# First sequence's softmax by token and its mix on TensorE, w_r loaded behind q, low parts of w_v and half of w_k made by accumulating transfers

## The chip, the cores and the metric

The kernel runs on one core of one Trainium2 chip. The metric is the device time of one execution in microseconds; a kernel's time is the median of several runs. Five engines work at once, each on its own instructions in a fixed order: TensorE (PE in the profile, with its weight loads as PEld), VectorE (DVE), ScalarE (ACT), GpSimd (POOL) and SyncE (SP), which issues most of the DMA transfers. They wait for each other by semaphores.

## The reference

Eight sequences of 576 tokens, eight heads of 64 channels. Each sequence has 32 packed queries `p`; an attention of `p` over `k` and `v` gives 32 packed values per head, and a second attention of `q` over these packed values gives the output of the attention. Its heads side by side are the 512 channels of `x`, which goes through a channel mix with a shift by one token.

```python
p_packed = sm_attn(p, k, v)               # softmax over 576 keys
x = sm_attn(q, p_packed, p_packed)        # softmax over 32 packed rows, (8, 576, 512)
x_prev = x shifted by one token, zero first
xk = mu_k * x + (1 - mu_k) * x_prev
xr = mu_r * x + (1 - mu_r) * x_prev
k = max(xk @ w_k, 0)                      # 512 -> 1024
v = k * k @ w_v                           # 1024 -> 512
out = 1 / (1 + exp(-(xr @ w_r))) * v
```

`mu_k`, `mu_r`, `w_k`, `w_v` and `w_r` come as 64-bit floats, the rest as 32-bit floats.

## The kernel before

**Order of work.** The kernel is written as generators ("parts") that yield what they need next: an engine with an estimated duration, a buffer slot, or an event. While the program is built, `Flow.run` takes the part that can start soonest by these estimates and, among equals, the one of lowest rank, and writes its instruction down. So each engine has a fixed order, made by a planner; on the chip only semaphores decide when an instruction starts. Ranks: 10 and up for the first sequence (less 1 for its second half), `RANK_MIX` 11.5 for the first block's mix, `RANK_W` 13.6 for w_r and w_k, 14.28 for the second sequence, `RANK_V` 15.2 for w_v, 30 and up for later sequences, 50 for the channel mix.

**Weights.** TensorE multiplies float32 in three products of rounded parts: high by high, high by low, low by high. `convert` (L268) brings one chunk of 128 rows by 512 columns of 64-bit words (512 KB) into a staging slot and makes the two parts: ACT reads the upper word (L286), DVE shifts and joins it with sign and lower word (L288, L290, L292), ACT rounds it to the high part (L296), DVE subtracts that from the word (L298) to get the low part. There are 4 chunks of w_r, 8 of w_k (columns 0 to 511 first, then 512 to 1023), 8 of w_v. Staging slots are borrowed from `sq`, at most four at a time (`staged`). The word lies in one of four `tmp` buffers until both parts are made.

**Attention.** For each sequence `loads` brings k, v and q in, four pairs of heads each. The first two sequences are transposed on TensorE (L394), later ones on DVE (L371). `front` (L435) computes the scores of `p` (L444), softmax (`weights_of`), the sum over v (L486 or L478) and `pm`, the packed values (L501). `back` (L617) does the second attention in two halves of 288 tokens: scores on TensorE (L611) with packed rows on partitions, a transpose on DVE in blocks of 32 (L635), maximum, subtraction, exponential, sum, reciprocal and product (L642 to L654), a transpose back (L658), and the product with `pm` (L666), copied by ACT to `xt` (L688), channels on partitions.

**Channel mix.** Tokens of all sequences in blocks of 512; block 0 holds tokens 0 to 511 of the first sequence, block 1 its last 64 and 448 of the second. `mix` (L707) makes xr or xk for 4 chunks of 128 channels: ACT multiplies `xt` by the share (L721), DVE multiplies the shifted `xt` and adds (L725); `split` rounds (ACT, L741) and subtracts (DVE, L743). Then on TensorE, per block: `gates` (48 matmuls of 128x512, L799 to L801, four token tiles, the next block's xr and all of w_r needed), `keys` (96, L760 to L762, eight groups f of 128 hidden channels, each over four chunks of xk and w_k), `squared` on ACT and DVE (L771 to L780), `values` (96, L828 to L830). `keep_busy` puts filler matmuls (L899) where TensorE would idle by plan, until the last gate tile of block 0. PSUM has two slots `pa` of two banks for the attention, and four slots `m` of one bank, of which one is the fillers' until then.

**Loads.** All go through SP in the planner's order (L207). The first two w_r chunks have ranks just behind the first sequence's loads (`FIRST`). `shares` (L869) loads `mu_k` and `mu_r`, one value per partition and chunk (L871), and makes one minus them (L875).

## Time and profile before

| what | value |
|---|---|
| median of 3 runs | 598.3 us (597.15 to 598.65) |
| the profiled execution's own time | 602.04 us |
| its span, first to last instruction | 600.3 us |
| mean granted TensorE clock | 0.997 |
| PE, PEld, DVE, ACT, POOL busy | 587.6, 465.4, 372.3, 317.4, 2.1 us |
| DMA traffic | 56.51 MB, 94 GB/s over the span |

One profiled execution gives all starts and durations. A row of the timeline has the start from the span's beginning, the duration, engine, line, operation, output and inputs, shapes and count; in brackets the idle time before it and what ended that. A row of groups has count, busy time, mean nanoseconds of one, and idle time before. Matmuls overlap their successors, so their durations add up to more than the time they take; their starts tell the pace. Four stages can be told apart: up to 44 us the first sequence and the weights, to 61 us the first block's gates, to 118 us its keys and values beside the second sequence, and then eight more blocks with the other sequences between them.

### The profile page before, as it was taken

The numbers are of one execution on the slowest core, as the hardware profiler recorded it, in microseconds if no ns is written. First come the engines' busy times: TensorE is split into PE (matmuls) and PEld (weight loads), VectorE is DVE, ScalarE is ACT, GpSimd is POOL, SyncE is SP. The second block draws the span as 40 slices with busy tenths as digits, with TensorE's granted clock in tenths as the row PEclk, the third lists the DMA queues.
The fourth block names the chain that finished last, engine by engine and source line by source line (L and its number), as shares of the span: only waits on it lengthen the run. The fifth ranks groups of instructions, "written<-read, shape, count | busy, mean of one in ns | idle before, by whom it ended". The sixth has DMA issues, their size and how long they took to land.

```text
span 600.3 us, 10117 instructions
## 1 busy us (share of the span) xinstructions
PE 587.6 (98%) x3924; PEld 465.4 (78%) x3924; DVE 372.3 (62%) x713; ACT 317.4 (53%) x555; POOL 2.1 (0%) x23
## 2 busy tenths in 40 slices
PE   9999999999999999998999999999999999999997
PEld 8777677787777777676777787778788888888886
DVE  1499999966779769745962977186404812551321
ACT  3578784863585675543833575257524703631410
POOL 0000000000000000000000000000000000000000
PEclk9999999999999999998999999999999999999999
DMA  8894661674665760764636343200100010001001
GB/s 194 250 281 120 218 149 42 141 168 84 143 135 130 155 137 15 186 142 70 133 82 166 89 77 93 79 0 1 58 13 1 1 70 1 0 1 70 1 0 71
DMA packets 170895, 56.51 MB, mean 94 GB/s; under 512 B 147808, under 2 KB 162144, under 8 KB 170848
## 3 DMA queue, kind: packets, MB, share of 16 engines
q1 hardware_dynamic: 170848, 55.87, 38.1%
q8 instruction: 31, 0.51, 0.3%
q14 instruction: 16, 0.13, 0.1%
HBM read 42.86 MB, written 12.98 MB: 93 GB/s over the span
## 4 chain that ended last, share of the span: by engine, by line
PE 80%; DVE 6%; SPq 5%; DMA 4%; ACT 2%; issue 2%; ACTq 0%; DVEq 0%
PE pvo L828 11%; PE pvo L830 11%; PE pvo L829 11%; PE ph L760 10%; PE ph L762 9%; PE ph L761 9%; SPq L207 5%; PE pr L799 4%; PE pr L801 4%; PE pr L800 4%; PE pa L666 2%; DVE m L290 2%; PE pa L611 1%; PE pa L478 1%; DMA vt<-in_v 1%
## 5 line engine op out<-in xcount | busy, mean ns | idle before, releaser
L760 PE MATMUL ph<-xk,wk_h 128*128 128x512 f32 x288 | 115.2, 400 | 0.0
L828 PE MATMUL pvo<-wv_h,sq 128*128 128x512 f32 x288 | 114.0, 396 | 0.0
L761 PE MATMUL ph<-xk,wk_h 128*128 128x512 f32 x288 | 112.7, 391 | 0.0
L762 PE MATMUL ph<-xk,wk_l 128*128 128x512 f32 x288 | 112.7, 391 | 0.0
L829 PE MATMUL pvo<-wv_l,sq 128*128 128x512 f32 x288 | 112.2, 390 | 0.0
L830 PE MATMUL pvo<-wv_h,sq 128*128 128x512 f32 x288 | 112.1, 389 | 0.0
L771 ACT ACTIVATE r<-ph 128x512 f32<-128x512 f32 x72 | 43.1, 598 | 93.5 <-PE ph L762 92.4
L778 DVE CAST sq<-r 128x512 fp32r<-128x512 f32 x72 | 30.2, 419 | 92.3 <-ACT r L774 89.9
L828 PEld LDWEIGHTS pvo<-wv_h,sq 128*128 128x128 f32 x288 | 54.0, 188 | 17.2 <-issue 6.3
L760 PEld LDWEIGHTS ph<-xk,wk_h 128*128 128x128 f32 x288 | 54.2, 188 | 16.2 <-issue 5.2
L725 DVE SCALAR_TENSOR_TENSOR x<-xt,mus,x 128x512 f32<-128x512 f32 (+7 forms) x128 | 60.4, 510 | 6.4 <-ACT x L721 6.2
L762 PEld LDWEIGHTS ph<-xk,wk_l 128*128 128x128 f32 x288 | 54.3, 189 | 11.6
L830 PEld LDWEIGHTS pvo<-wv_h,sq 128*128 128x128 f32 x288 | 54.1, 188 | 11.5
L829 PEld LDWEIGHTS pvo<-wv_l,sq 128*128 128x128 f32 x288 | 54.1, 188 | 10.7
L761 PEld LDWEIGHTS ph<-xk,wk_h 128*128 128x128 f32 x288 | 54.3, 188 | 10.3
L721 ACT ACTIVATE x<-xt,mus 128x512 f32<-128x512 f32 (+7 forms) x128 | 61.5, 528 | 1.3 <-DVE xr L743 1.3
L801 PE MATMUL pr<-wr_h,xr 128*128 128x512 f32 x144 | 56.5, 393 | 1.0 <-DVE xr L743 1.0
L799 PE MATMUL pr<-wr_h,xr 128*128 128x512 f32 x144 | 56.8, 395 | 0.0
L800 PE MATMUL pr<-wr_l,xr 128*128 128x512 f32 x144 | 56.1, 390 | 0.0
L810 ACT ACTIVATE sig<-pr 128x512 f32<-128x512 f32 x36 | 21.5, 600 | 60.5 <-PE pr L801 60.4
L780 DVE TENSOR_TENSOR sq<-r,sq 128x512 fp32r<-128x512 f32 x72 | 49.3, 685 | 1.4
L774 ACT ACTIVATE r<-r 128x512 f32<-128x512 f32 x72 | 45.5, 631 | 1.7
(85 smaller groups left out, 681.3 us busy)
## 6 DMA issues: line engine op xcount, KB each, us to landing
out<-sig SPq DMA_DIRECT2D x36, 256.0 KB, 2.5
vt<-in_v SPq DMA_DIRECT2D x16, 512.0 KB, 4.5
raw<-in_k SPq DMA_DIRECT2D x96, 72.0 KB, 2.7
raw<-in_q SPq DMA_DIRECT2D x96, 72.0 KB, 2.8
st<-in_moe_w_k SPq DMA_DIRECT2D x8, 512.0 KB, 6.2
st<-in_moe_w_v SPq DMA_DIRECT2D x8, 512.0 KB, 5.6
far<-at SPq DMA_DIRECT2D x12, 288.0 KB, 2.3
aTd<-far SPq DMA_DIRECT2D x12, 256.0 KB, 2.9
```

Of the source, the lines that this page charges most:

```text
L721: nc.scalar.mul(x32[:, o:o + n], xts[b, c][:, 1 + s:1 + s + n], mus[:, j, c:c + 1])
L725: nc.vector.scalar_tensor_tensor(x32[:, o:o + n], xts[b, c][:, s:s + n], mus[:, j + 1, c:c + 1], x32[:, o:o + n], op0=ALU.mult, op1=ALU.add,)
L760: nc.tensor.matmul(ph, wk_h[:, c, fs], xh, start=(c == 0), stop=False)
L761: nc.tensor.matmul(ph, wk_h[:, c, fs], xl, start=False, stop=False)
L762: nc.tensor.matmul(ph, wk_l[:, c, fs], xh, start=False, stop=(c == NC - 1))
L780: nc.vector.tensor_tensor(hl[:, 1, :], r, hl[:, 0, :].bitcast(F32), op=ALU.subtract)
L799: nc.tensor.matmul(pr, xh[:, ts_], wr_h[:, c, :], start=(c == 0), stop=False)
L800: nc.tensor.matmul(pr, xh[:, ts_], wr_l[:, c, :], start=False, stop=False)
L801: nc.tensor.matmul(pr, xl[:, ts_], wr_h[:, c, :], start=False, stop=(c == NC - 1))
L828: nc.tensor.matmul(pv[t], sh, wv_h[:, f, :], start=(f == 0), stop=False)
L829: nc.tensor.matmul(pv[t], sh, wv_l[:, f, :], start=False, stop=False)
L830: nc.tensor.matmul(pv[t], sl, wv_h[:, f, :], start=False, stop=(f == NF - 1))
```

## The change

It concerns the start of the kernel.

- **By token.** The first sequence's second attention is computed with tokens on partitions (`by_token`): q is the stationary operand, `both` holds the packed rows of a pair of heads on the diagonal, and the scores of 128 tokens come as 256 columns. `weights_by_token` does the softmax in windows of 256, 256 and 64 tokens without the DVE transposes, then transposes on TensorE and copies to `A0`, with a zero column ahead.
- **Mixed on TensorE.** `shared` multiplies `pm` by the shares of each channel and by one minus them; `first_mix` then gets xr and xk directly as two accumulated products, of `A0` and of `A0` one token earlier. ACT rounds from PSUM, DVE subtracts from PSUM, 256 columns at a time. The last 64 tokens are kept in float32 for block 1 (`kept`), where `mix` copies them.
- **Gates of block 0** run two token tiles side by side over the chunks, so they need only the first 256 tokens at first; the fillers end ahead of the second two.
- **Loads.** All four chunks of w_r come right behind the first sequence's q; the staging area is a pool `st` of eight slots of its own, without the limit of four. The parts of w_v stay in these slots. The q of the first sequence goes through `sq` slots. The shares are loaded by POOL's queue, once repeated over 32 partitions for `shared`, and later by rows with a transpose on TensorE for the other blocks.
- **Low parts by transfer.** For w_v and the second half of w_k the subtraction L298 goes: ACT writes minus the high part, and a transfer from POOL's queue adds the word to it in place.
- **Waits.** w_k's conversion waits for the third window; the third sequence's front waits for the second sequence's `px`.

The core of the diff:

```diff
-    FIRST = 10.09, 10.29
+    FIRST = 10.05, 10.06, 10.07, 10.08
...
-                pa=2, both=1, m=4, staged=4)
+                pa=2, both=1, m=4, st=NF)
...
-        staged = yield from flow.take("staged")
-        slot = yield from flow.take("sq")
+        slot = yield from flow.take("st")
...
+        if held:
+            yield from flow.wait(("A", 2))
...
         nc.vector.scalar_tensor_tensor(m, w0, 29, m, op0=ALU.logical_shift_right, op1=ALU.bitwise_or)
-        flow.give("sq", slot)
-        flow.give("staged", staged)
+        if hi is None:
+            wv = wvs[c] = tile_([P, 2, DM], F32R, "st", slot, "wv")
+            h, l = wv[:, 0, :], wv[:, 1, :]
+        else:
+            h, l = hi[:, c, o:o + n], lo[:, c, o:o + n]
+            flow.give("st", slot)
         yield act(n)
-        nc.scalar.copy(hi[:, c, o:o + n], m.bitcast(F32))
-        yield vec(n)
-        nc.vector.tensor_tensor(lo[:, c, o:o + n], m.bitcast(F32), hi[:, c, o:o + n].bitcast(F32), op=ALU.subtract)
+        nc.scalar.copy(h, m.bitcast(F32))
+        if event[0] == "wk" and o or event[0] == "wv":
+            yield act(n)
+            nc.scalar.activation(l, h.bitcast(F32), AF.Copy, scale=-1.0)
+            yield "gpsimd", 1.0, None, None
+            nc.gpsimd.dma_start(l, m.bitcast(F32), accum_op=ALU.add)
+            flow.now.t += 2.5
+            yield from reached()
+        else:
+            yield vec(n)
+            nc.vector.tensor_tensor(l, m.bitcast(F32), h.bitcast(F32), op=ALU.subtract)
         flow.give("tmp", sm)
...
+    WINDOWS = (0, 256), (256, 256), (TB, S - TB)
+    def by_token(sb2, both):
...
+                for pr in range(NPR):
+                    nc.tensor.matmul(
+                        s2[:n, j, :, 32 * pr:32 * pr + 32], ts["qT", 0, pr][1][:, t:t + n], both[:, :, pr, :],
+                        start=True, stop=True,
+                    )
+    def weights_by_token(w, blocks, slot, s2):
...
+        nc.vector.tensor_reduce(m2, sc, axis=AX.X, op=ALU.max)
+        nc.vector.tensor_tensor(e, sc, m2.unsqueeze(3).broadcast_to([n, nb, 8, 32]), op=ALU.subtract)
+        nc.scalar.activation(e, e, AF.Exp, scale=scale)
+        nc.vector.tensor_reduce(z2, e, axis=AX.X, op=ALU.add)
+        nc.vector.tensor_scalar_add(z2, z2, eps)
+        nc.vector.reciprocal(z2, z2)
+        nc.vector.tensor_tensor(e, e, z2.unsqueeze(3).broadcast_to([n, nb, 8, 32]), op=ALU.mult)
...
+                nc.tensor.transpose(
+                    tp[:, h, j * P:j * P + n], e[:, j, 4 * h:4 * h + 4].rearrange("p a b -> p (a b)"), ident[:n, :n],
+                )
...
+        nc.scalar.copy(parts["A0"][:, :, 1 + t:1 + t + total], tp[:, :, :total])
+    def shared(sp, pm):
...
+        for j in (1, 0):
+            nc.vector.tensor_tensor(pms[:, j, 0], flat, mub[1][:, j], op=ALU.mult)
+            nc.vector.tensor_tensor(pms[:, j, 1], flat, pms[:, j, 0], op=ALU.subtract)
+    def first_mix():
...
+        for tag, j, w in (("xr", 1, 0), ("xr", 1, 1), ("xk", 0, 0), ("xk", 0, 1), ("xr", 1, 2), ("xk", 0, 2)):
...
+            for g in range(2):
+                for tap in range(2):
+                    for pr in (2 * g, 2 * g + 1):
+                        own = slice(32 * pr, 32 * pr + 32)
+                        for h, half in enumerate(HALVES):
+                            o = 1 - tap + t
+                            nc.tensor.matmul(
+                                px[half, pr % 2, :n], pms[own, j, tap, h * D:(h + 1) * D], A[own, h, o:o + n],
+                                start=(tap == 0), stop=(tap == 1),
+                            )
...
+            nc.scalar.copy(tiles[c][:, 0, cols], px[:, c % 2, :n])
+        nc.vector.tensor_tensor(tiles[c][:, 1, cols], px[:, c % 2, :n], tiles[c][:, 0, cols].bitcast(F32), op=ALU.subtract)
...
     def gates(i):
-        for t in range(NT):
+        for t in range(0, NT, STEP if i == 0 else 1):
...
+                if t == STEP:
+                    flow.keep_busy = 0.0
+                    flow.give("m", 3)
...
-                flow.spawn(convert(w_k, wk_h, wk_l, c, o, WP, ("wk", c, o)), RANK_W)
+                flow.spawn(convert(w_k, wk_h, wk_l, c, o, WP, ("wk", c, o), held=True), RANK_W)
...
-                flow.spawn(convert(w_v, wv_h, wv_l, f, o, WP, ("wv", f, o)), RANK_V)
+                flow.spawn(convert(w_v, None, None, f, o, WP, ("wv", f, o)), RANK_V)
```

More of the change, by code (lines that the diff above doesn't have):

```diff
@@ L264, in attn_pack_channel_mix, with convert @@
     wr_l = const.tile([P, NC, DM], F32R, name="wr_l")
-    wv_h = const.tile([P, NF, DM], F32R, name="wv_h")
-    wv_l = const.tile([P, NF, DM], F32R, name="wv_l")
-    def convert(w, hi, lo, c, o, n, event, first=None):
+    wvs = {}
+    def convert(w, hi, lo, c, o, n, event, first=None, held=False):
         rank = flow.now.rank
@@ L437, in front @@
         yield from flow.wait(("pt", b), *(("kT", b, pr) for pr in range(NPR)))
+        if b == 2:
+            yield from flow.wait(("px", 1, 0), ("px", 1, 1))
         slots = yield from two_slots()
@@ L507, in front @@
         nc.tensor.transpose(pT[:, :P], pm.rearrange("p a b -> p (a b)"), ident)
+        if b == 0:
+            s2 = yield from flow.take("a2")
+            both = tile_([P, 2, NPR, 32], F32, "a2", s2, "ppB")
+            nc.gpsimd.memset(both, 0.0)
+            yield act(2 * P)
+            for h, own in enumerate(HALVES):
+                nc.scalar.copy(both[own, h], pT[own, :P].rearrange("p (r x) -> p r x", x=32))
+            flow.give("pa", slot)
+            flow.spawn(shared(sp, pm), RANK_MIX)
+            parts["A"] = yield from flow.take("xt")
+            A = parts["A0"] = tile_([P, 2, S + 1], F32, "xt", parts["A"], "A0")
+            nc.gpsimd.memset(A[:, :, 0:1], 0.0)
+            flow.spawn(by_token(s2, both), rank(b) - 1)
+            return
         ppT = sb.tile([P, P], F32, name="ppT", tag="ppT")
@@ new lines, in shared @@
+    def shared(sp, pm):
+        yield from flow.wait("mub")
+        ss = yield from flow.take("sig")
+        parts["pms"] = ss
+        pms = parts["pm"] = tile_([P, 2, 2, 2 * D], F32, "sig", ss, "pms")
+        flat = pm.rearrange("p a b -> p (a b)")
+        for j in (1, 0):
+            yield vec(P)
+            nc.vector.tensor_tensor(pms[:, j, 0], flat, mub[1][:, j], op=ALU.mult)
+            yield vec(P)
+            nc.vector.tensor_tensor(pms[:, j, 1], flat, pms[:, j, 0], op=ALU.subtract)
+        flow.give("pm", sp)
+        flow.give("sig", mub[0])
+        flow.set("pms")
@@ new lines, in first_out @@
+    def first_out(tag, j, w, g, slot, px, tiles, kept):
+        t, n = WINDOWS[w]
+        if w == 2:
+            yield act(2 * n)
+            nc.scalar.copy(kept[:, j, 2 * g:2 * g + 2, :], px[:, :, :n])
+            flow.give("pa", slot)
+            flow.set(("kept", j, g))
+            return
+        cols = slice(t, t + n)
+        for c in (2 * g, 2 * g + 1):
+            yield act(n)
+            nc.scalar.copy(tiles[c][:, 0, cols], px[:, c % 2, :n])
+            flow.spawn(first_low(tag, w, c, tiles, cols, slot, px, n), flow.now.rank)
@@ L711, in mix @@
         for c in range(NC):
-            yield from flow.wait(*(("xt", b, c, hf) for b, *_ in pieces(i) for hf in range(2)))
+            yield from flow.wait(*(
+                e for b, *_ in pieces(i)
+                for e in ([("xt", b, c, 0), ("xt", b, c, 1)] if b else [("kept", j // 2, c // 2)])
+            ))
             slot = yield from flow.take("xk" if tag == "xk" else "sq")
-            space = "sig" if i == 0 else "tmp"
+            space = "tmp"
             sx = yield from flow.take(space)
@@ L720, in mix @@
                 yield act(n, after=ready)
+                if not b:
+                    nc.scalar.copy(x32[:, o:o + n], parts["keep"][:, j // 2, c, :])
+                    continue
                 nc.scalar.mul(x32[:, o:o + n], xts[b, c][:, 1 + s:1 + s + n], mus[:, j, c:c + 1])
@@ L748, in attn_pack_channel_mix, with made @@
     sqs, sigs = {}, {}
+    def made(tag, i, c, t=NT - 1):
+        if i:
+            return [(tag, i, c)]
+        return [(tag, 0, c, hf) for hf in range(1 + (t >= 2))]
     def keys(i):
@@ L867, in all_loads @@
             yield from loads(b)
+    mub = []
     def shares():
-        for j, mu in ((0, mu_k), (2, mu_r)):
-            yield from load(mus[:, j, :], mu.rearrange("(c p) -> p c", p=P), 0.46, 0.23)
-            if not j:
-                back_to_issue()
+        yield from flow.wait(("kT", 0, NPR - 1))
+        sm = yield from flow.take("sig")
+        mub[:] = sm, tile_([P, 2, 2 * D], F32, "sig", sm, "mub")
+        for j, mu in ((0, mu_k), (1, mu_r)):
+            for pr in range(NPR):
+                yield from load(
+                    mub[1][32 * pr:32 * pr + 32, j, :],
+                    mu[2 * D * pr:2 * D * (pr + 1)].unsqueeze(0).broadcast_to([32, 2 * D]), 0.46, 0.05, beside=True,
+                )
+        flow.now.t += 2.5
+        flow.set("mub")
+        yield from flow.wait(("A", 2))
+        sr = yield from flow.take("tmp")
+        by_row = tile_([2 * NC, P], F32, "tmp", sr, "by_row")
+        for j, mu in ((0, mu_k), (1, mu_r)):
+            yield from load(by_row[NC * j:NC * (j + 1), :], mu.rearrange("(c p) -> c p", p=P), 0.46, 0.05, beside=True)
+        flow.now.t += 2.5
+        yield from reached()
+        slot = yield from flow.take("pa")
+        pT = banks(slot).rearrange("p a b -> p (a b)")
+        yield pe(0.1)
+        nc.tensor.transpose(pT[:, :2 * NC], by_row, ident[:2 * NC, :2 * NC])
+        flow.give("tmp", sr)
+        yield act(2 * NC)
+        nc.scalar.copy(mus[:, 0::2, :], pT[:, :2 * NC].rearrange("p (a b) -> p a b", a=2))
+        flow.give("pa", slot)
         yield vec(2 * NC)
```

148 lines of the change are left out of this document (115 added, 33 removed).

## The prediction

> **What bounds the kernel now.** I read the page's busy times and its 40 slices first, then busy time by stretches, then the timelines of PE and DVE.
>
> ```profile
> PE 587.6 (98%) x3924; PEld 465.4 (78%) x3924; DVE 372.3 (62%) x713; ACT 317.4 (53%) x555; POOL 2.1 (0%) x23
> DVE  1499999966779769745962977186404812551321
> 22.50:44.10 21.60, 20.39 (x221) 18.07 (x221) 20.72 (x39) 14.94 (x26) 0.00 (x0) 1.00 0.96 276
> 44.10:52.60 8.50, 7.52 (x49) 5.69 (x48) 8.50 (x15) 8.50 (x16) 0.00 (x0) 1.00 0.56 133
> 52.60:61.00 8.40, 8.40 (x38) 6.92 (x39) 8.23 (x15) 5.59 (x9) 0.00 (x0) 1.00 0.43 133
> 61.00:93.10 32.10, 30.52 (x276) 23.05 (x275) 30.73 (x62) 25.79 (x48) 0.00 (x0) 1.00 0.66 184
> 93.10:118.00 24.90, 24.90 (x161) 18.74 (x160) 24.76 (x51) 15.45 (x31) 0.10 (x1) 1.00 0.34 75
> ```
>
> A stretch's row gives its length, the busy time of PE, PEld, DVE, ACT and POOL, the granted clock, the DMA share and GB/s. PE is busy 98% of the span, so the time moves only if work leaves PE or if its real work begins sooner. Before 44 us PE is busy with fillers (L899) and short attention matmuls, while DVE has no room: 20.72 of 21.60 us, then 8.50 of 8.50. **DVE sets the start and PE sets the rest.** PE's timeline shows the handover:
>
> ```profile
> 45.80 0.50 PE L801 MATMUL pr<-wr_h,xr 128*128 128x512 f32 x1 [0.97 <-DVE xr L743]
> 52.80 0.39 PE L799 MATMUL pr<-wr_h,xr 128*128 128x512 f32 x1
> 60.98 0.39 PE L760 MATMUL ph<-xk,wk_h 128*128 128x512 f32 x1
> 63.02 0.39 PE L760 MATMUL ph<-xk,wk_h 128*128 128x512 f32 x1
> 70.01 1.20 PE L444 MATMUL pa<-kT,pt 64*32 64x288 f32 x32 [1.38 <-DVE pt L423]
> 93.13 0.39 PE L828 MATMUL pvo<-wv_h,sq 128*128 128x512 f32 x1
> 118.04 0.39 PE L799 MATMUL pr<-wr_h,xr 128*128 128x512 f32 x1
> ```
>
> The first gate tile (12 matmuls) is stretched by waits for the mixed inputs, the other 36 run from 52.80 to 60.98, which is 0.227 us each; 48 would take 10.9 us. From 60.98 the keys run without a gap except for 1.38 us at 70.01. So a change is worth what it moves the keys' start and what it does to the gaps behind it.
>
> **The change, part by part.** First the work that DVE does before the keys can start:
>
> ```profile
> L725 DVE SCALAR_TENSOR_TENSOR x<-xt,mus,x 128x512 f32<-128x512 f32 x8 | 5.8, 747 | 0.0
> L743 DVE TENSOR_TENSOR xk<-x,xk 128x512 fp32r<-128x512 f32 x4 | 2.7, 687 | 0.0
> L743 DVE TENSOR_TENSOR xr<-x,xr 128x512 fp32r<-128x512 f32 x4 | 2.7, 686 | 0.0
> L658 DVE STREAM_TRANSPOSE a<-e 128x576 f32<-128x576 f32 x2 | 1.5, 770 | 0.0
> ...
> L650 DVE TENSOR_SCALAR z<-z 128x18 f32<-128x18 f32 x2 | 0.3, 143 | 0.0
> 59.39 0.42 DVE L288 TENSOR_SCALAR m<-m 128x512 uint32<-128x512 uint32 x1
> ...
> 61.18 0.68 DVE L298 TENSOR_TENSOR wk_l<-m,wk_h 128x512 fp32r<-128x512 f32 x1
> 61.78 0.42 DVE L288 TENSOR_SCALAR m<-m 128x512 uint32<-128x512 uint32 x1
> ```
>
> The groups are DVE's between 22.5 and 61.8 us (count, then busy us, mean ns, idle before); the eight from L658 to L650 are the first sequence's softmax, 9.4 us together. One weight chunk takes 61.78 - 59.39 = 2.39 us, of which its low part L298 is 0.60 (starts lie some 0.08 us closer than the busy times say). The low part of the last w_k chunk of the first half ends at 61.78, and the matmul that reads it follows at 63.02: DVE is 1 us ahead of PE here, so both set the start.
>
> *Softmax by token* drops the two transposes of each half. Two reduces and two tensor operations of 0.75 us on 576 columns become 0.67 on 512, so a window of 256 tokens costs 4 x 0.67 + 0.4 for the small ones = 3.1, the last 64 tokens half of that: 7.7 against 9.4, **-1.7 us**. *Mixing on TensorE* drops L725 for the first block: 8 x 0.67 = **-5.3**. The subtractions stay, as 16 on 256 columns instead of 8 on 512. No row shows that form; I halve 0.60 and add 0.04 for the fixed part, 16 x 0.34 = 5.4 against 4.8: **+0.6** (0 to +4.8, if half the columns cost as much as all). *Scaling pm by the shares* is four operations on 128x128, some 1.1 us in all; it fits the 2.50 us in which DVE waits for the first weights (below): 0, or +1.1 without that cover. *w_r behind q* takes the loads of the shares from between the second and third chunk:
>
> ```profile
> 18.16 5.86 DMA mus<-in_moe_mu_k
> 23.17 0.43 DVE L288 TENSOR_SCALAR m<-m 128x512 uint32<-128x512 uint32 x1 [2.50 <-ACT m L286]
> 27.33 0.67 ACT L286 ACTIVATE m<-st 128x512 f32<-128x512 f32 x1 [1.63 <-DMA st<-in_moe_w_r]
> ```
>
> The third chunk may land some 2 us sooner, but DVE idles for only 0.9 us of its first stretch, and that not only for this: -0.3. **DVE: -1.7 - 5.3 + 0.6 - 0.3 = -6.7**, so the keys start at 54.3 instead of 60.98. Ends: -2.5 where the half-size subtractions save nothing, -8 where PE takes over, as follows.
>
> PE must be ready by then. It gets eight groups of mix matmuls of 256 columns and four of 64:
>
> ```profile
> 34.81 0.74 PE L666 MATMUL pa<-a,pm 32*64 32x288 f32 x16 [0.87 <-DVE a L658]
> ```
>
> Sixteen of these on four row groups took 0.74; a mix group has eight on two row groups, so I take 0.65 (0.33 if the row groups did not matter), in all about 6 us. Nearly all of it takes the place of fillers. The gates need w_r, which DVE finishes around 23.2 + 4 x 2.4 (w_r) + 7.7 (softmax) + 5.4 (subtractions) = 46. Two gate tiles, fed chunk by chunk, end 1.4 us later, the other two 5.5 us after that: 53. So PE's bound (53) lies just under DVE's (54.3), and no more than 8 us can be had. The k transposes of the second sequence (L394, eight of 0.33) are free before 40 us now; four more weight chunks go ahead of their loads, 2 MB at 276 GB/s = 7.6 us, so some come behind the gates: +0.7 (0 to +2.6). The gap of 1.38 us at 70.01 hangs on one place in DVE's order and may not come again: -0.7 (0 to -1.4). These two cancel.
>
> ACT loses the multiplications and gets twelve copies and sixteen half-size casts in place of eight whole ones:
>
> ```profile
> L721 ACT ACTIVATE x<-xt,mus 128x512 f32<-128x512 f32 x8 | 5.6, 719 | 0.0
> ```
>
> It was busy 14.94 of 21.60 us, so it does not bound. That w_k's conversion now waits for the softmax's last window costs nothing, as it stands behind w_r and that window on DVE anyway.
>
> *Low parts by transfers* takes 12 x 0.60 = 7.2 us off DVE behind the start and gives ACT 12 copies of about 0.52, with 6.3 us idle from 61 to 93.1 and 9.5 from there to 118. DVE's gain is not on the path, yet needed: the second block's gates at 118.04 must come 6.7 us sooner too, and DVE is busy 24.76 of 24.90 us there. With 6.7 + 7.2 us less in front, it can follow. The price is the transfer; the trace has none of this kind, so its ends are the nearest rows:
>
> ```profile
> far<-at SPq DMA_DIRECT2D x12, 288.0 KB, 2.3
> st<-in_moe_w_k SPq DMA_DIRECT2D x8, 512.0 KB, 6.2
> 68.44 0.68 DVE L292 SCALAR_TENSOR_TENSOR m<-st,m 128x512 uint32<-128x512 uint32 x1
> 78.03 0.40 PE L762 MATMUL ph<-xk,wk_l 128*128 128x512 f32 x1
> 109.69 0.68 DVE L298 TENSOR_TENSOR wv_l<-m,wv_h 128x512 fp32r<-128x512 f32 x1
> ```
>
> I take 2.5 us to land, by the row of its size, and 1 us to issue. What matters first is the last w_k chunk of the second half. Its word is done at 69.1 (L292); less 6.7, less three L298 ahead of it, that is 60.6; two copies make it 61.7, the transfer 65.2, or 69 by the slow row. The matmul that reads it (78.03) comes at 71.3. It is covered by 2 to 6 us, so 0. Behind a late one stand all later matmuls, in order, and ACT and DVE, since a transfer holds one of four tmp buffers until it lands.
>
> The loads of the shares on POOL's queue (ten small ones, one transpose, one copy) and the new wait of the third sequence's front cost nothing: POOL is busy 2.1 us in all, and that front's L444 comes behind the second sequence's L666 now too.
>
> One rule speaks against the transfers. DVE's fast forms run at nearly half the time of the others:
>
> ```profile
> L778 DVE CAST sq<-r 128x512 fp32r<-128x512 f32 x8 | 3.3, 417 | 0.1
> L288 DVE TENSOR_SCALAR m<-m 128x512 uint32<-128x512 uint32 x11 | 4.6, 418 | 0.0
> ```
>
> The Trainium skill, "SBUF — State Buffer", section "Who interferes with whom", says that copies, casts and tensor_scalar of this kind can lock GpSimd out of the port through which it writes the descriptors of its own DMAs, for the whole instruction. By it each transfer could start up to 0.42 us later per such instruction that it meets, and the sum would stay, as the cover above is larger. No run here shows a GpSimd transfer yet.
>
> **Sum.** -6.7 + 0.7 - 0.7 = -6.7. The profiled execution took 602.04 us with a span of 600.3, so 593.6 of span; the median of the runs is 598.3, and the same step gives **591.6 us**. Its own range is 587 to 594.5: down to -8 on the start, the gap of 1.4 gone too, and 2 us of a later gap (shown below); up where the half-size subtractions lose half of their 4.2 us and the transposes 0.7.
>
> **Rivals.** *Late low parts (595 to 597).* With the loads of w_v beside them and the tmp buffers held, the last of the four lands 11.5 us after its issue: 74.2 against 71.3, so PE waits some 3 us, and its clock falls, as it does now behind three gaps at 269 to 273:
>
> ```profile
> 272.89 0.30 PE L478 MATMUL pa<-vl,aTd 64*32 64x64 f32 x4 [1.00 <-DMA aTd<-far]
> 272.00:274.00 2.00, 1.11 (x7) 0.88 (x8) 0.73 (x3) 0.00 (x0) 0.00 (x0) 0.86 0.56 86
> 274.00:276.00 2.00, 2.00 (x14) 1.05 (x20) 0.59 (x1) 0.27 (x1) 0.00 (x0) 0.50 0.74 115
> 276.00:278.00 2.00, 2.00 (x34) 0.97 (x35) 0.80 (x2) 0.00 (x0) 0.00 (x0) 0.78 0.60 95
> ```
>
> The lost clock is 0.28 + 1.00 + 0.44 = 1.7 us; 591.6 + 3 + 1.7 = 596.3. For it: DMA is at 0.66 of its time from 61 to 93 us. Against: the cover of 2 to 6 us.
>
> *The second sequence holds (597 to 599).* Its loads come 7.6 us later, its q stays where it is, and the second block's gates stay at 118; the gain is given back as a wait there. For it: DVE is full up to 118. Against: DVE is relieved of 13.9 us.
>
> *Slower (603): the transfers run one at a time.* Twelve begin at about 57 us; the last w_v chunk is read at 93.13 + 7 x 2.72 = 112.2, so at 105.5 after the change. With t us for each, PE waits if 57 + 12 t is over 105.5 (t = 4.0) and the kernel is slower from t = 4.6. At 5 us it is 11.5 - 6.7 = 4.8 us slower: 603.1. For it: 512 KB landed in 6.2 us. Against: 288 KB landed in 2.3, and DMAs of SP overlap in this trace; and weight loads that were issued half a microsecond apart overlap in this trace. With 13.9 us less on DVE, the last word of w_v is ready about 96 us (109.69 + 0.6 now), its low part about 101, some 4 us before it is read.
>
> **Chances.** Forecast 0.64, late low parts 0.14, second sequence 0.08, slower 0.11, better than 587 by luck in the later order 0.03. The range takes in all but the slower case and the lucky one: 587 to 599. Faster by over 0.3% (1.8 us, about what a measurement of this kernel can tell from no change) is below 596.5: 0.64 + 0.03 + 0.14 = 0.81; within it, the second sequence's case, 0.08; slower 0.11.
>
> **What would show it.** Right: L760's first matmul near 54, the first sequence's mix on DVE gone, its subtractions near 0.34 us, the second block's first gate near 111, and no PE wait on an input that a transfer wrote. Wrong: 256-column subtractions near 0.6; keys waiting on wk_l; values waiting on wv_l; a gap of PE ahead of the second block's gates with clock under 1.

## The result and the profile after

The kernel became slower: 607.61 us median (606.91 to 607.77, 4 runs) against 598.47 (597.15 to 599.15, 4 runs). The ratio is 1.0146, 95% interval 1.0127 to 1.0166. The profiled execution took 607.48 us with a span of 605.7 and a mean clock of 0.993. The forecast was 591.6.

The busy times of the page after show that DVE was relieved as meant (372.3 us before), and that PE stayed the bound:

```profile
PE 588.6 (97%) x3989; PEld 461.9 (76%) x3989; DVE 360.6 (60%) x699; ACT 318.9 (53%) x573; POOL 18.0 (3%) x45
```

The same stretches as before, by busy time (PE, PEld, DVE, ACT, POOL, then clock, DMA share, GB/s):

```profile
22.50:44.10 21.60, 21.57 (x219) 16.89 (x219) 19.41 (x45) 11.39 (x26) 1.03 (x2) 1.00 0.80 269
44.10:52.60 8.50, 8.50 (x94) 5.05 (x96) 6.54 (x15) 5.58 (x13) 0.00 (x0) 1.00 0.44 131
61.00:93.10 32.10, 28.86 (x238) 21.95 (x238) 21.70 (x43) 26.24 (x50) 5.61 (x7) 0.95 0.92 227
93.10:118.00 24.90, 24.90 (x187) 17.80 (x184) 23.98 (x44) 18.72 (x39) 5.07 (x9) 1.00 0.54 103
```

Two things are to be seen. From 44.1 to 52.6 us it is now PE that has no room (8.50 of 8.50) and DVE that has (6.54): the bound of the start has changed hands. And from 61 to 93.1 us PE and DVE are idle more than before: PE 28.86 where it was 30.52, DVE 21.70 where it was 30.73, with the clock at 0.95. ACT is a little busier, with its twelve new copies (26.24 where it was 25.79). The DMA share, which is the time of the packets as a share of 16 engines and goes over 1 in some rows below, went from 0.66 to 0.92.

PE's timeline gives the places (the first key, two gaps, then the second block's first gate; the idle time and what ended it are in brackets):

```profile
56.97 0.47 PE L950 MATMUL ph<-xk,wk_h 128*128 128x512 f32 x1
...
77.75 0.47 PE L409 MATMUL pa<-ident,raw 96*128 96x96 f32 x3 [3.08 <-ACT a L581]
...
121.86 0.50 PE L1025 MATMUL pvo<-wv,sq 128*128 128x512 f32 x1 [3.75 <-DMA wv<-m]
```

The keys start at 56.97, 4.0 us sooner than the 60.98 of before. The second block's gates start at 126.08, 8.0 us later than 118.04, and 15 us later than the forecast 111. So 12.0 us are lost between these two points. Both gaps pull the clock down behind them (each row begins with stretch and length; the clock stands third from the end):

```profile
78.00:80.00 2.00, 2.00 (x11) 1.62 (x10) 0.95 (x3) 2.00 (x6) 0.00 (x0) 0.56 0.36 145
80.00:82.00 2.00, 2.00 (x10) 1.60 (x9) 0.61 (x1) 1.10 (x2) 0.61 (x1) 0.58 0.35 79
...
122.00:124.00 2.00, 2.00 (x7) 1.55 (x8) 0.91 (x2) 1.17 (x3) 0.10 (x1) 0.66 0.50 79
124.00:126.00 2.00, 2.00 (x6) 1.61 (x5) 1.16 (x2) 0.00 (x0) 0.00 (x0) 0.50 0.81 179
```

The lost clock is 2.00 x (0.44 + 0.42) = 1.7 us and 2.00 x (0.34 + 0.50) = 1.7 us. Idle times of PE between the two points add up to 7.7 us, where before they were 1.6 (the 1.38 at 70.01 and 0.20): +6.1. Transposes of the second sequence's k, summed from start to next start over the timeline, take 1.1 us there, since they now stand among the keys (to 63 us) and no longer at 31 to 40; another 0.7 us of them stand just ahead of the first key. Together 6.1 + 3.4 + 1.1 = 10.6 of the 12.0; the rest is spread over many matmuls.

**Who made the first gap.** PE waited for ACT's exponential (L581) of the second sequence. ACT's timeline shows why it came so late:

```profile
66.36 0.62 ACT L302 CAST wk_h<-m 128x512 fp32r<-128x512 f32 x1
67.52 0.60 ACT L961 ACTIVATE r<-ph 128x512 f32<-128x512 f32 x1 [0.55 <-DMA wk_l<-m]
...
69.90 0.60 ACT L961 ACTIVATE r<-ph 128x512 f32<-128x512 f32 x1 [0.74 <-DMA wk_l<-m]
...
73.19 0.66 ACT L288 ACTIVATE m<-st 128x512 f32<-128x512 f32 x1 [2.02 <-DMA wk_l<-m]
...
75.57 1.28 ACT L581 ACT_TABLE_LOAD   x1
76.87 0.74 ACT L581 ACTIVATE a<-pa,nmx 128x576 f32<-128x576 f32 x1
```

L961 takes the keys out of PSUM and L288 begins the next weight chunk; neither reads wk_l. What they need is one of the four `tmp` buffers, and a transfer holds it until it has landed. Three such waits are 3.3 us, and the exponential stands behind them in ACT's order. No matmul waits for wk_l itself in this trace. The transfers' own rows (size, median us from issue to landing):

```profile
wv<-m POOLq DMA_DIRECT2D x8, 256.0 KB, 3.7
wk_l<-m POOLq DMA_DIRECT2D x4, 256.0 KB, 6.0
```

The plan allows 1.0 us of POOL and 2.5 to land. **The second gap** is the last transfer of w_v itself: it was issued at 115.87, and the matmul that reads it waited until 121.86. Two things made it late, by some 2 us each. ACT had written its high part by 112.6, but the minus high part only at 114.95, behind the second block's mix. And this transfer took 5.9 us to land, where the seven before it took 3.2 to 3.9.

### The profile page after: what moved, and what is told of

It is laid out like the page before. It is cut to its first block, busy times and chain, and to the rows that moved or that the text cites. A ratio compares the mean times of both kernels' runs of the same rounds, so it can differ in the third digit from the quotient of the medians.

```text
span 605.7 us, 10333 instructions
## 1 busy us (share of the span) xinstructions
PE 588.6 (97%) x3989; PEld 461.9 (76%) x3989; DVE 360.6 (60%) x699; ACT 318.9 (53%) x573; POOL 18.0 (3%) x45
## 4 chain that ended last, share of the span: by engine, by line
PE 79%; DMA 6%; DVE 5%; SPq 4%; issue 3%; ACT 3%; POOL 0%; DVEq 0%; POOLq 0%; ACTq 0%
PE ph L950 10%; PE ph L951 9%; PE ph L952 9%; PE pvo L1024 9%; PE pvo L1025 9%; PE pvo L1026 9%; PE pr L994 5%; PE pr L996 5%; PE pr L995 5%; SPq L211 4%; DMA raw<-in_q 2%; PE pa L820 1%; PE pa L496 1%; PE pa L700 1%; PE spare L1120 1%
## 5 line engine op out<-in xcount | busy, mean ns | idle before, releaser
L1025 PE MATMUL pvo<-wv,sq 128*128 128x512 f32 x288 | 113.1, 393 | 3.8 <-DMA wv<-m 3.8
L1024 PE MATMUL pvo<-wv,sq 128*128 128x512 f32 x288 | 114.8, 399 | 0.0
L1026 PE MATMUL pvo<-wv,sq 128*128 128x512 f32 x288 | 112.8, 392 | 0.0
L961 ACT ACTIVATE r<-ph 128x512 f32<-128x512 f32 x72 | 43.0, 597 | 89.1 <-PE ph L952 87.5
L1024 PEld LDWEIGHTS pvo<-wv,sq 128*128 128x128 f32 x288 | 54.3, 189 | 18.0 <-issue 6.3
L1025 PEld LDWEIGHTS pvo<-wv,sq 128*128 128x128 f32 x288 | 54.4, 189 | 14.8 <-DMA wv<-m 4.1
L1026 PEld LDWEIGHTS pvo<-wv,sq 128*128 128x128 f32 x288 | 54.5, 189 | 11.6
L905 DVE SCALAR_TENSOR_TENSOR x<-xt,mus,x 128x448 f32<-128x448 f32 (+6 forms) x112 | 53.1, 513 | 7.1 <-ACT x L899 6.9
L899 ACT ACTIVATE x<-xt,mus 128x448 f32<-128x448 f32 (+6 forms) x112 | 54.2, 528 | 1.3 <-DVE xr L927 1.3
L1035 DVE TENSOR_TENSOR sig<-pvo,sig 128x512 f32<-128x512 f32 x36 | 24.0, 687 | 39.6 <-PE pvo L1026 39.6
```

Of the source, the lines that this page charges most:

```text
L899: nc.scalar.mul(x32[:, o:o + n], xts[b, c][:, 1 + s:1 + s + n], mus[:, j, c:c + 1])
L905: nc.vector.scalar_tensor_tensor(x32[:, o:o + n], xts[b, c][:, s:s + n], mus[:, j + 1, c:c + 1], x32[:, o:o + n], op0=ALU.mult, op1=ALU.add,)
L1024: nc.tensor.matmul(pv[t], sh, wvs[f][:, 0, :], start=(f == 0), stop=False)
L1025: nc.tensor.matmul(pv[t], sh, wvs[f][:, 1, :], start=False, stop=False)
L1026: nc.tensor.matmul(pv[t], sl, wvs[f][:, 0, :], start=False, stop=(f == NF - 1))
```

## The experiments

Theory A: the transfers cost the time, by the buffer that each holds while it lands. Rivals: the sums come too late for the matmuls that read them (B); the rest of the change costs it, the start or the second sequence (C). All times are medians; each ratio is to the kernel before, run beside it on the same chip. Medians of different rows come from different chips, so small differences between rows are read from the ratios.

| kernel | low parts by transfer | median us | ratio and interval |
|---|---|---|---|
| after | half w_k, w_v | 607.6 | 1.0146 (1.0127 to 1.0166) |
| e1 | none | 599.1 | 1.0010 (0.9982 to 1.0038) |
| e2: before, with transfers | half w_k, w_v | 614.7 | 1.0232 (1.0171 to 1.0293) |
| e3: 6.0 us planned to land | half w_k, w_v | 620.8 | 1.0353 (1.0293 to 1.0414) |
| e4 | w_v | 600.8 | 1.0026 (1.0004 to 1.0049) |
| e5 | half w_k | 602.9 | 1.0054 (1.0034 to 1.0074) |
| e6: e1, held by plain copies | none | 602.5 | 1.0047 (1.0023 to 1.0071) |
| e7: w_v loaded later | half w_k, w_v | 603.5 | 1.0060 (1.0037 to 1.0082) |
| e8: e1, second k first | none | 604.5 | 1.0076 (1.0057 to 1.0095) |
| e9: w_k's words in `sq` | half w_k, w_v | 608.2 | 1.0154 (1.0133 to 1.0176) |
| **e9b: e5, words in `sq`** | half w_k | **596.9** | **0.9949 (0.9925 to 0.9973)** |
| e11: e1, second sequence first | none | 606.3 | 1.0122 (1.0090 to 1.0153) |
| e12: all words in `sq` | half w_k, w_v | 604.9 | 1.0111 (1.0088 to 1.0135) |
| e13: e9, w_v loaded later | half w_k, w_v | 604.8 | 1.0097 (1.0075 to 1.0119) |

Every edit also makes the planner place other instructions anew, so differences of a microsecond or two can come from the new order alone: with the same start, the first key lies at 54.73 in e12 and at 58.04 in e3. The verdicts below rest on rows that name a wait.

### The transfers, and the change without them

e1 subtracts on DVE everywhere and keeps the rest:

```diff
-        if event[0] == "wk" and o or event[0] == "wv":
+        if False:
```

> The changed kernel with every low part subtracted on DVE again, no transfers. Theory A (the transfers: their landing holds the tmp buffers that ACT needs, and the last one of w_v lands late): PE's gaps of 3.1 us at 77.75 and 3.8 us at 121.9 and the half clock behind each (1.8 and 1.9 us) go; DVE's 7.2 us more fit where it idles 10.4 of 32.1 us: about 597 us (595.5 to 599), second block's first gate near 116. Theory B (the second sequence comes too late, through its loads behind four more weight chunks): the gate stays near 126 and the time at 605 to 608.

e2 is the kernel before with nothing but the transfers put into its `convert`:

```diff
-        nc.vector.tensor_tensor(lo[:, c, o:o + n], m.bitcast(F32), hi[:, c, o:o + n].bitcast(F32), op=ALU.subtract)
+        if event[0] == "wk" and o or event[0] == "wv":
...
+            nc.scalar.activation(lo[:, c, o:o + n], hi[:, c, o:o + n].bitcast(F32), AF.Copy, scale=-1.0)
...
+            nc.gpsimd.dma_start(lo[:, c, o:o + n], m.bitcast(F32), accum_op=ALU.add)
...
+        else:
...
+            nc.vector.tensor_tensor(lo[:, c, o:o + n], m.bitcast(F32), hi[:, c, o:o + n].bitcast(F32), op=ALU.subtract)
```

> The kernel before with the transfers alone (w_v and half of w_k), nothing else of the change. Theory A: the same waits for tmp and for the last low part, 603 to 608 us. Theory B: the transfers cost nothing by themselves and only relieve DVE, 596 to 599 us.

e1 took 599.1, so the transfers cost some 8 us (8.5 by the medians), and the rest of the change brings nothing by itself that can be told from noise. Neither gap is there: the longest idle times of PE in e1 between its keys and its second block's gates are 0.67 and 0.44 us. In e2 the transfers alone cost 2.3%, some 14 us (15.6 by the medians), and the same wait stands there, longer: first ACT's copy of the keys out of PSUM, then PE's waits (the row has the total, the count and the longest).

```profile
71.97 0.60 ACT L779 ACTIVATE r<-ph 128x512 f32<-128x512 f32 x1 [4.36 <-DMA wk_l<-m]
```
```profile
PE pa L402 <- ACT a L556: 6.1, 1, 6.1
```

There wk_l took 9.3 us to land (median). Rival C is out for the loss, but C is right about the missing gain; it is taken up again below.

### Is it the planner's estimate?

```diff
-            flow.now.t += 2.5
+            flow.now.t += 6.0
```

> The changed kernel with the planner told that a transfer takes 6.0 us instead of 2.5 before its buffer is free; same work, other order. Theory A in the form that the order trusted too short a landing: ACT no longer stands behind a transfer while others could go, gaps shrink, 599 to 603 us. Theory A in the form that the buffers are simply too few: 605 to 609. Theory B: 605 to 608, with the gate at 126 as now.

620.8: a truer estimate makes it worse. The planner moves the work elsewhere, and PE then waits 3.9 us for DVE, 3.4 for wv and 3.2 for DVE. So a truer number in the plan doesn't mend it; another order with the same number was not tried.

### Which transfers?

e4 keeps the transfers of w_v alone, e5 those of w_k alone:

```diff
-        if event[0] == "wk" and o or event[0] == "wv":
+        if event[0] == "wv":
```
```diff
-        if event[0] == "wk" and o or event[0] == "wv":
+        if event[0] == "wk" and o:
```

> The changed kernel with transfers for w_v only; the second half of w_k is subtracted on DVE. Theory A: the first gap (3.1 us and 1.8 of clock, behind the wk_l transfers) goes and the last one (3.8 and 1.9) may stay: about 602 us (600 to 604). Theory B: 605 to 608.

> The changed kernel with transfers for the second half of w_k only; w_v is subtracted on DVE. With none it takes 599.1 us, with w_v's 600.8, with both 607.6. If the four w_k transfers are what costs (they took 6.0 us to land beside the loads of w_v, and ACT waited 3.3 us for their buffers): 603 to 607 us, with PE's gap before 78 us there again. If only both together cost, by the sum of buffers held: 599 to 602.

By the ratios, w_v alone costs 0.16% over e1, some 1 us and within the intervals; w_k alone 0.44%, some 2.6 us; the two together 1.36%, some 8, more than their sum. With w_k alone the first gap is back, behind the same instruction of ACT:

```profile
74.68 0.66 ACT L288 ACTIVATE m<-st 128x512 f32<-128x512 f32 x1 [2.50 <-DMA wk_l<-m]
```
```profile
79.25 0.74 PE L409 MATMUL pa<-ident,raw 96*128 96x96 f32 x3 [4.05 <-ACT a L581]
```

Behind this gap the clock lies at 0.50 from 78 to 84 us. With w_v alone ACT's longest wait for a transfer is 0.55 us, and this gap is not there.

### Holding the buffer, without a sum

e6 is e1 with a plain copy of the same twelve words to device memory; `tmp` is given back only when the copy has landed. Nothing reads the copies.

```diff
+        flow.set(event)
+        if event[0] == "wk" and o or event[0] == "wv":
+            sink = dram.tile([P, WP], U32, name="sink", tag=f"sink{event[0]}{c}")
+            yield "gpsimd", 1.0, None, None
+            nc.gpsimd.dma_start(sink, m)
+            flow.now.t += 2.5
+            yield from reached()
         flow.give("tmp", sm)
-        flow.set(event)
```

> Every low part is subtracted on DVE, but for w_v and half of w_k a plain transfer from POOL's queue copies the word to device memory and holds its tmp buffer until it lands; nobody reads the copy. Theory of the held buffer: the waits of ACT come back without any low part being late, 603 to 608 us. Theory of the late low part (PE and the tiles' readers wait for the sum itself): as without transfers, 598 to 600 us.

602.5, by the ratios some 2 us over e1: between the two forecasts. The four copies of w_k's words landed in 4.4 to 5.5 us, where the sums took 5.2 to 7.9, and ACT waited only 1.2 us for one of them. So the run didn't hold the buffers as long as the sums do, and it doesn't decide between A and B.

### Is the slow landing due to the loads of w_v?

```diff
+        if hi is None:
+            yield from flow.wait(("wk", NC - 1, WP))
         slot = yield from flow.take("st")
```

> The changed kernel, transfers kept, with w_v's 512 KB loads held back until w_k is done. If the w_k transfers land late because the loads share the DMA engines with them: landing falls from 6.0 to 3 to 4 us, ACT's 3.3 us of waits and the gap before 78 us go, and the time is 601 to 605 us unless w_v then comes late itself. If landing is the transfer's own time: 6 us again, 607 us or more.

The median landing of wk_l stayed at 6.7 us. But the loads were not gone: the new wait stands in the planner's order, and on the chip four of them were issued while w_k's transfers, issued from 61.39 to 68.30, were still under way. SP's rows, of after and then of e7:

```profile
66.60 3.76 SPq L211 DMA_DIRECT2D st<-in_moe_w_v  x5
```
```profile
65.54 2.59 SPq L211 DMA_DIRECT2D st<-in_moe_w_v  x4
```

From 62 to 76 us the DMA share is 1.13 in both kernels. So this run doesn't test the question. The traces of all runs, transfer by transfer, say more (landing from issue, and the DMA share over the 6 us from the issue):

| transfers | issued at | landing, us | DMA share |
|---|---|---|---|
| after, wk_l | 62.21, 64.60, 66.54, 68.94 | 5.3, 5.2, 6.6, 7.9 | 1.17, 1.20, 1.16, 1.10 |
| e9 and e12, first wv | 68.97, 70.48 | 8.2, 7.4 | 1.14, 1.08 |
| e13, first three wv | 81.89, 83.58, 85.20 | 5.9, 7.6, 6.7 | 1.10, 1.17, 1.14 |
| after, two wv | 97.12, 105.06 | 3.2, 3.2 | 0.28, 0.34 |
| e6, copies of w_k's words | 59.86, 62.73, 64.52, 67.39 | 4.9, 5.5, 4.4, 5.4 | 1.03, 1.15, 1.10, 1.02 |
| e6, last three copies | 93.65, 95.44, 104.84 | 2.3, 2.3, 2.3 | 0.22, 0.11, 0.37 |

Where the DMA engines are full, w_v's transfers are as slow as w_k's, so the slow landing goes with the stretch and not with the tensor. It isn't a strict rule (a wv of e13, issued at 109.94, landed in 4.1 at a share of 1.16), and which of the other transfers matters was not tested.

The time fell to 603.5 all the same, and the gap of 3.08 became 0.45. Here no chunk of w_v is there to be begun, so the L288 that waited 2.02 us no longer stands ahead of the exponential, which runs at 72.75 instead of 76.87. That speaks for A: the landing is as slow and the gap is gone. With the gap gone, a matmul waits for the last of w_k's sums itself, which B expects, though only for a short time:

```profile
76.58 0.50 PE L954 MATMUL ph<-xk,wk_l 128*128 128x512 f32 x1 [0.58 <-DMA wk_l<-m]
```

### The buffer taken away

Here the landing is left as it is and only the held buffer is changed, apart from what the planner places anew. In e9 the word of a transferred w_k chunk lies in one of the eight `sq` buffers, some of which are free between the first block's gates and its squares. e9b does the same to e5.

```diff
-        sm = yield from flow.take("tmp")
-        m = tile_([P, WP], U32, "tmp", sm, "m")[:, :n]
+        space = "sq" if event[0] == "wk" and o else "tmp"
+        sm = yield from flow.take(space)
+        m = tile_([P, WP], U32, space, sm, "m")[:, :n]
...
-        flow.give("tmp", sm)
+        flow.give(space, sm)
```

> The changed kernel, but the word of w_k's second half lies in one of the eight sq buffers until its transfer has landed, no longer in one of the four tmp buffers. Theory (the transfer holds the tmp buffer, ACT waits for it, and behind ACT the second sequence's exponential is late): landing stays near 6 us, ACT's waits for wk_l among the keys (0.55 + 0.74 + 2.02 = 3.3 us) go below 0.5, PE's gap of 3.08 behind the exponential goes below 0.8 and with it the 1.8 us of lost clock; about 603 instead of 607.6, the rest being the wait of 3.8 for w_v. Rival (the sums themselves come too late for the keys): PE waits 2 us or more on wk_l itself, and the time stays at 606 to 608.

> As e5 (transfers for w_k's second half alone, 602.9 us), with the word in an sq buffer as in e9. Theory of the held buffer: the gap of 4.05 us behind the exponential goes, and the time comes to the 599 of the kernel that subtracts everywhere. Rival: a gap of 3 us or more stays, on wk_l or elsewhere, and the time stays at 602 to 604.

e9b is the run that decides: 596.9 instead of the 602.9 of e5 (0.9949 and 1.0054 of before), with the transfers nearly as slow (6.8 in e5):

```profile
wk_l<-m POOLq DMA_DIRECT2D x4, 256.0 KB, 6.4
```
```profile
70.83 0.60 ACT L962 ACTIVATE r<-ph 128x512 f32<-128x512 f32 x1 [0.23 <-DVE nmx L578]
71.46 0.63 ACT L965 ACTIVATE r<-r 128x512 f32<-128x512 f32 x1
72.11 1.28 ACT L582 ACT_TABLE_LOAD   x1
73.41 0.74 ACT L582 ACTIVATE a<-pa,nmx 128x576 f32<-128x576 f32 x1
```

ACT has no wait on a transfer here, the exponential runs at 73.41 (78.37 in e5), and no gap of PE up to the second block's gates is over 0.89 us. The sums land 6.4 us after their issue (median) and no matmul waits for them. The margin is small: the last one is issued at 67.15, 2.8 us sooner than in e5, lands 6.8 us later, and is read at 75.56. In e5 too no matmul waits for wk_l, only one weight load, for 0.4 us. **For w_k the cost is the held buffer, not the late sum;** a late sum comes to 0.58 us in e7. This kernel is also faster than before, by 0.5% (0.27 to 0.75), and so beats both.

e9 missed its number (608.2 against some 603), and its rows say why:

```profile
77.23 0.60 ACT L962 ACTIVATE r<-ph 128x512 f32<-128x512 f32 x1 [4.35 <-DMA wv<-m]
```

With w_k's words out of `tmp`, the planner let w_v's first conversions go ahead; their transfers took `tmp` (the first was issued at 68.97, in after at 81.39), and ACT's copy of the keys out of PSUM, ahead of the exponential, waited for them. The gap of PE behind the exponential was 3.72 us.

### w_v's part

e12 puts the words of all twelve in `sq` (its line against that of e9). e13 is e9 with the edit of e7.

```diff
-        space = "sq" if event[0] == "wk" and o else "tmp"
+        space = "sq" if event[0] == "wk" and o or event[0] == "wv" else "tmp"
```

> The changed kernel with the words of all twelve transfers in sq buffers, none in tmp. Theory (w_v's transfers too cost by the tmp buffer they hold while ACT needs it for the keys): ACT's waits for a transfer go below 0.5 us in all, there is no gap of PE behind the second sequence's exponential near 78 us, and the time is 596 to 600, as e9b. Rival (w_v's sums land too late, or its words now wait for an sq buffer behind the squares): PE waits 2 us or more on wv or on the squares between 95 and 125 us; 603 or more.

> The kernel of e9 (w_k's words in sq, w_v's in tmp) with w_v's loads held until the last chunk of w_k's second half is done, as in e7. Theory of the held buffer: no w_v transfer stands beside the second sequence's exponential, ACT waits under 1 us among the keys, the gap of 3.7 us near 80 goes and the time is 598 to 601. Rival (twelve transfers cost several us wherever their words lie): the gaps come back at the values or ahead of the second block's gates, and the time is 603 or more.

Both missed the theory's 596 to 601 and came out at some 605. In e12 ACT no longer waits for a transfer among the keys, but DVE does: its rounding of the squares needs an `sq` buffer, and transfers of w_k and w_v hold them. The exponential came at 76.82, and PE's gap behind it was still there.

```profile
66.20 0.43 DVE L969 CAST sq<-r 128x512 fp32r<-128x512 f32 x1 [2.82 <-DMA wk_l<-m]
...
77.98 0.43 DVE L969 CAST sq<-r 128x512 fp32r<-128x512 f32 x1 [2.06 <-DMA wv<-m]
...
87.07 0.43 DVE L969 CAST sq<-r 128x512 fp32r<-128x512 f32 x1 [0.66 <-DMA wv<-m]
```
```profile
77.71 0.66 PE L410 MATMUL pa<-ident,raw 96*128 96x96 f32 x3 [2.01 <-ACT a L582]
```

In e13 the gap of 3.7 at 80 us is gone as expected. But ACT waits 1.63 and 1.20 us for transfers of w_v at 87.86 and 91.22, and the values wait, once for ACT and twice for w_v itself:

```profile
95.45 0.50 PE L1027 MATMUL pvo<-wv,sq 128*128 128x512 f32 x1 [1.59 <-ACT r L964]
...
107.95 0.50 PE L1028 MATMUL pvo<-wv,sq 128*128 128x512 f32 x1 [1.37 <-DMA wv<-m]
112.03 0.50 PE L1028 MATMUL pvo<-wv,sq 128*128 128x512 f32 x1 [1.06 <-DMA wv<-m]
```

So both A and B seem to have a share for w_v: the wait follows whichever pool lends the buffer, and where it is pushed back, the sums come too late. How much each takes of the 3.8 us at 121.86 is not settled.

### Where the gain of the start went

e1 has the earlier keys and no transfers, yet equals the kernel before. Two kernels tried to bring its second sequence forward: e8 loads its k ahead, into `sq`; e11 ranks its attention ahead of the conversions.

```diff
-    RANK_1, RANK_MIX, RANK_W, RANK_V, LOADS_1 = 14.28, 11.5, 13.6, 15.2, 14.29
+    RANK_1, RANK_MIX, RANK_W, RANK_V, LOADS_1 = 14.28, 11.5, 13.6, 15.2, 13.55
...
-                space = ("xk" if tag == "kT" else "sq") if b == 0 else "raw"
+                space = ("xk" if tag == "kT" else "sq") if b == 0 else "sq" if b == 1 and tag == "kT" else "raw"
```
```diff
-    RANK_1, RANK_MIX, RANK_W, RANK_V, LOADS_1 = 14.28, 11.5, 13.6, 15.2, 14.29
+    RANK_1, RANK_MIX, RANK_W, RANK_V, LOADS_1 = 13.3, 11.5, 13.6, 15.2, 14.29
```

> No transfers (as e1_subtract_all, 599.1 us), and the second sequence's k loads go ahead of w_k, into staging slots that the mix leaves free, so that its k transposes run before the keys and not among them. Theory that PE is the bound from 34 us and these 2.7 us of transposes are part of what ate the gain of the start: second block's first gate 2 to 3 us sooner than 115.4, time 596 to 597.5. Rival, that DVE and the weights behind these loads set the keys' start: keys later by up to 4 us, time 599 to 602.

> The kernel of e1 (all low parts subtracted, 599.1 us), with the rank of the second sequence's attention set ahead of the conversions of w_k and w_v (14.28 becomes 13.3). Theory (the start's gain is lost because the second block's mix comes late, held by the second sequence's attention behind ACT and DVE): its weights' matmuls (S2) come 4 us or more before 92.0, the second block's gates run without gaps (11 instead of 12.2 us) and the time is 595 to 597. Rival (DVE is full whatever the order): S2 stays at 91 or later, or w_k's second half comes late instead and PE waits among the keys; 599 or more.

Both were slower than e1. The scores of the second sequence's first and second attention, in PE's timeline of e1:

```profile
64.53 1.20 PE L462 MATMUL pa<-kT,pt 64*32 64x288 f32 x32
...
91.99 1.20 PE L645 MATMUL pa<-qT,ppT 64*32 64x288 f32 x32
```

and of before, whose first scores are quoted in the prediction at 70.01:

```profile
90.51 1.20 PE L611 MATMUL pa<-qT,ppT 64*32 64x288 f32 x32
```

In e1 the chain begins 5.5 us sooner and passes this point 1.5 us later. DVE is full there (busy time of e1; before has 19.82 of the same 20.00):

```profile
86.00:106.00 20.00, 20.00 (x170) 14.60 (x176) 20.00 (x41) 8.48 (x16) 0.00 (x0) 1.00 0.13 22
```

In e8 this point came at 95.92 and in e11 at 96.27: a better place in the plan's ranks didn't bring it forward. The exponential already ran late, at 77.86 and 77.30 (72.99 in e1), so neither kernel made the condition that its theory needs. And the second block's mixed inputs were late (gaps of PE of 1.32 and 0.83 us on `xr` in e8, 1.28 and 1.24 in e11). In e9b, where four subtractions fewer stand on DVE, it comes at 88.61. So the lead shrinks as follows, by the starts of the first key, the second block's first key and the fourth block's first gate: e1 is 4.4, 1.3 and 0.6 us ahead of before, e9b 4.4, 2.0 and 2.4. The last figures roughly fit the medians, 0.0 and 2.4. That DVE alone holds the chain was argued from its full row and from e9b, and is not shown: in e8 DVE was busy 18.85 of the 20.00 us, and the chain came later all the same.

### Before, once more

> The kernel before, once more, for a second profile. If the gaps of 0.80 and 1.00 us near 271 us and the lost clock behind them belong to the one profiled execution (602.0 against a median of 598.3), the start of the fifth block's gates comes some 4 us sooner than 312.72, near 308.5, and the span is near 596.5; then the 4.4 us that e1 is ahead at the keys are given back by 181 us. If they stand in every execution, it starts near 312.7 again and the span is 600.

The fifth block's gates start at 312.96, as in the second case. The second profile (602.3 us) has the stall of the first again, 0.74 and 1.40 us in place of 0.80 and 1.00:

```profile
270.84 0.65 PE L478 MATMUL pa<-vt,aTd 128*32 128x64 f32 x32 [0.74 <-DMA aTd<-far]
273.13 0.30 PE L478 MATMUL pa<-vl,aTd 64*32 64x64 f32 x4 [1.40 <-DMA aTd<-far]
```

Of sixteen other executions of before, timed on the same chip, eleven lay between 597.7 and 599.5 and five from 601.1 to 604.8, so both profiled ones are among the longer ones of this kernel. Whether the stall stands in the shorter ones too, no profile shows, and differences should be read ahead of 271 us. That is why the spans of before and after differ by 5.4 us and the medians by 9.1: at the fourth block's gates, ahead of that place, after is 253.08 - 244.91 = 8.2 us late.

## Why the prediction was wrong

- **The step that failed** is the cost of the transfers: "I take 2.5 us to land", "It is covered by 2 to 6 us, so 0." Two things were wrong in it. The landing was mis-sized: in after w_k's four took 5.2 to 7.9 us and w_v's eight 3.2 to 5.9. And the cover was counted for the matmul that reads the sum alone. That part nearly held (no wait in after, where the exponential holds PE up anyway, none in e9b, 0.58 us in e7). What the sum left out was named one line below, "a transfer holds one of four tmp buffers until it lands", and was given no term of its own. The four words of w_k, in a pool of four that also takes the keys out of PSUM, cost ACT 3.3 us, PE 3.1 and the clock 1.7. The rival "late low parts" had the right size of gap and clock (3 + 1.7), and it named the held buffers, but its price was for the wrong path, PE on wk_l instead of PE on ACT on a buffer, and only once; w_v's gap is a second one (3.75 + 1.7).
- **How much of the miss this is.** Between the forecast of 591.6 and the 607.6 of after lies e1 with 599.1: some 8 us are the transfers, and some 7 are the start's forecast gain, of which e1 had 4.4 at its first key and gave it back.
- **The rival "slower"** expected transfers one at a time, slower than before from 4.6 us each. The time, 607.6, lies beyond its 603, but its place was wrong: w_k's transfers cost through a buffer, and the last one of w_v was late since ACT wrote its input late and it landed slowly itself.
- **The start** gained 4.0 us, not 6.7. The term that was mis-sized is the mix on TensorE: "so I take 0.65", some 6 us in all. One group took 1.02 (start to next start) and a short one 0.39: 8 x 1.02 + 4 x 0.39 = 9.7 us. The rule behind 0.65 compared eight matmuls with the sixteen of L666, but the trace holds two records for each matmul of this kind, whose operands are not rounded (the keys, with rounded operands, leave one: 288 for 9 x 8 x 4):

```profile
L820 PE MATMUL pa<-A,pms 32*64 32x256 f32 x128 | 7.7, 386 | 0.0
L820 PE MATMUL pa<-A,pms 32*64 32x64 f32 x64 | 1.8, 229 | 0.0
```

  The program has 8 x 8 = 64 of the first form and 32 of the second. L666's sixteen were eight as well. The place was wrong too: "Nearly all of it takes the place of fillers". The last filler ends where the first gate begins, at 34.91, and from there to the first key PE has no gap. Of these 22.1 us the 48 gate matmuls at 0.227 are 10.9, six long and four short groups 7.7 and transposes 1.1; the rest, 2.4, is a slower pace where PE changes from one kind to the other (0.31 to 0.34 us to the next start instead of 0.23). So PE bounds the start, as the row of 44.1 to 52.6 shows too. That 53 + 3.7 = 56.7 lies so near 56.97 is partly luck, since the 53 let the gates begin when DVE is done with w_r, at 46.
- **ACT** was called free by its first stretch, although the row of the second had it full (8.50 of 8.50). It did no harm: after the change it is busy 5.58 us there.
- **DVE's terms** held roughly: the transposes and L725 of the first block are gone. The subtractions of 256 columns took 0.42 us, not 0.34, 1.3 us in all, which no longer counts behind PE:

```profile
L844 DVE TENSOR_TENSOR xr<-pa,xr 128x256 fp32r<-128x256 f32 x8 | 3.1, 416 | 0.7 <-ACT xr L839 0.6
```

- **The k transposes** were put at 0.7 (0 to 2.6) and took 1.1 among the keys and 0.7 just ahead of them. The gap of 1.38 at 70.01 was gone, as forecast.
- **"With 6.7 + 7.2 us less in front, it can follow"** was not borne out. Without the 7.2 (e1) the second block's lead was 1.3 us at its keys, with a third of it (e9b) 2.0; no run has all of it without the waits for transfers. The rival "second sequence holds" (597 to 599) describes e1's 599.1 well; it had 0.08.
- The rule of the Trainium skill on DVE and GpSimd's descriptors ("SBUF — State Buffer", "Who interferes with whom") was not tested by itself; no run tells it apart as a cause of the landing of 6.0 us. The rows beside it were read a little too well: the fast forms take 417 and 418 ns against some 685, which is 0.6 of the others' time and not nearly half.

## What to carry to other kernels

A transfer that replaces an engine's instruction must be priced twice: for who reads its result, and for what it holds until it lands. Count the pool's buffers, the instructions on other engines that take from the same pool meanwhile, and what stands behind those in order; the profile shows such a wait as an instruction that waits for a DMA whose data it never reads. When an operation is sized by a neighbour's row, count the program's instructions in both, not the rows of the trace. And when a run is meant to take something away, look in its trace whether it is gone: the loads of e7 were not.

## What the runs showed of the hardware

Accumulating transfers of one size, 256 KB from POOL's queue, had medians of 3.7 to 4.6 us for w_v, and of 5.8 to 9.3 for w_k, which were issued where the DMA share was mostly over 1; plain copies to device memory had 3.4. Single ones took from 3.2 us (at a share of 0.28) to 9.6. The Trainium skill, "DMA: Bandwidth & Descriptors", section "Anatomy of one DMA — SWDGE (gpsimd) path", gives 2.0 us and the bytes at 436 GB/s, by which 256 KB would be an estimated 2.6; every accumulating transfer here is above that, and only plain copies at a low share came below it, at 2.3.

An idle PE of 3.08 us was enough to bring the clock to 0.56 for about 4 us. The Trainium skill, "TensorE: Matmul & The Clock Gate", Part 1, lets the clock fall after an idle window of some 3.4 us: the gap of 3.75 agrees, while the one of 3.08, that of 2.01 in e12 (clock 0.50 from 78 to 80 us), and above all the two of 0.80 and 1.00 at 271 us of before, show that less can do. The length alone doesn't decide: a gap of 1.95 us at 70.27 in the second profile of before left the clock at 1.00.
